# Gate and up weights of a fused S5 scan and gated MLP, loaded slot by slot over 128 partitions

## Chip, cores and metric

One core of one Trainium2 chip. The metric is the device time of one execution in microseconds; lower is better. Engines: PE is TensorE, DVE VectorE, ACT ScalarE, POOL GpSimd, SP SyncE, which computes nothing and issues most DMAs.

## What is computed

2048 tokens of 448 features are normalised; one branch is a diagonal complex recurrence (S5), the other a gated MLP, and both are multiplied and added to the input.

```python
xn = _layernorm(x)                                   # 2048 x 448
# S5: B_bar = ((Lam_bar - 1) / Lam) * (B_re + 1j B_im), 448 x 448
Bu = einsum("bld,pd->blp", xn, B_bar)
h[t] = Lam_bar * h[t-1] + Bu[t]
s = 2 * einsum("blp,dp->bld", h, Cmat).real + xn * Dskip
# MLP: w_gate, w_up 448 x 1792, w_down 1792 x 448
hid = sigmoid(xn @ w_gate) * (xn @ w_up)
g = silu(hid @ w_down)
out = x + s * g
```

All inputs and the output are bfloat16.

## The kernel before

**Tiling.** The tokens are 16 tiles of 128 (x tiles 0 to 15), worked in four chunks of 512. For a chunk the normalised x is transposed, features on partitions: chunk 0 on TensorE, chunks 1 to 3 by DMA transposes issued from SyncE. 448 features are seven slots of 64 rows. `wgt["g"]` and `wgt["u"]` (wG and wU in the profile) hold w_gate and w_up as [128 partitions, 7 slots, 896 columns]: partitions 0 to 63 hold the left 896 of the 1792 columns, partitions 64 to 127 the right 896, and slot s the feature rows 64 s to 64 s + 63. The 896 columns are seven column groups m of 128.

**The MLP's first products.** `gu_mm(c, k, m, ...)` (line 797) makes one column group of one chunk: for each of seven steps a pair of matmuls with 64 rows each, one on the lower partitions with slot s, one on the upper with slot s + 1 (modulo 7). `gu_evac` takes gate groups through a tanh on ACT, and up groups through a product on DVE (line 844) into hF. For chunk 0 the gate groups 0 and 1 are made tile by tile (`last_tile`, lines 825 and 826), then gate groups 2 to 6, then up groups 0 to 6, then the B products of the recurrence.

**Loads.** They stand in SyncE's queue in the order of the code: the x tiles 0 to 3 (two of them on ACT's queue), four loads of gate groups 0 and 1 (`load_w0`), then `load_w` for the rest. One `load_w` covers 64 partitions, seven slots and two or three column groups; groups 2 to 6 of the gate are four such loads (lines 418 to 421), the up weights are six (lines 432 to 438), with x tiles 4, 5 and 6, 7 between them. Then come four DMA transposes of B (`b_load`, line 742: for the real and the imaginary part one of 384 rows into bT 0 to 2, key bT, and one of 128 rows into bT 3, key bT3), dbc (the skip vector), the four transposes of chunk 1, w_down, the transposes of C, x tiles 8 to 15. GpSimd copies parts of bT into bT6 and bT's slot 3 (lines 746 to 754).

**B products.** `b_phase(c)` (line 870) makes four column groups. `pairs` are matmuls on slot 3 alone (bT3), `fulls` on slots 0 to 2; the group pt = 3 reads bT6 in place of bT.

**Order.** The program records every operation with its engine, an estimated cost and the keys it reads and writes; `Plan.solve` simulates backward and forward and emits the operations in order of planned start. TensorE's and the loads' order is as written (`chain`); DVE, ACT and POOL are ordered by the plan. `land` is the landing time that the plan assumes for a load, `HEAD_DMA` the number of DMAs at the head for which a fixed place among eight semaphores is assumed: DMA n waits for the landing of DMA n - 8. None of this sets a time on the chip; it sets the order. The waits between instructions follow from what each reads and writes: a matmul waits for the loads of the bytes that it reads.

**The end.** `yout` makes an output tile of a chunk in acc, DVE finishes it, `store` sends it from SyncE; `last_yout` is the last tile.

The new weight keys of the change are ("w", k, "s", s), one for a slot; `wkeys` (line 381) names what a column group reads for the plan.

Of the kernel before, what the change touches and what calls it, by code (L numbers as in the profile page):

```python
# [18 lines left out]
D = 448  # L19
F = 1792  # L20
P = 128
H = 64
# [4 lines left out]
TPC = L // P  # L27
NTAB = L + 1
EPS = 1e-5
HEAD_DMA = 19  # L30
TWO_PI = 2.0 * math.pi
PI = math.pi
MAGIC = 12582912.0
# [213 lines left out]
def kernel(  # L247
# [18 lines left out]
    V, A, G, T, Q = nc.vector, nc.scalar, nc.gpsimd, nc.tensor, nc.sync  # L266
# [99 lines left out]
    def load_w(eng, k, half, b, r=(), rate=105e3, land=0.0):  # L366
        m0, m1 = BLK[k][b]
        ps = slice(half * H, half * H + H)
        c0 = half * 896
        load(eng, [("w", k, half, m) for m in range(m0, m1)], H * 7 * (m1 - m0) * P * 2,  # L370
             wgt[k][ps, :, m0 * P:m1 * P],
             wsrc[k][:, c0 + m0 * P:c0 + m1 * P].rearrange("(s p) f -> p s f", p=H), cost=0.65, r=r, rate=rate, land=land)

    def load_w0(eng, half, part, r=(), land=0.0):
        ps = slice(half * H, half * H + H)
        s0, c0 = (1 - half if part == "A" else half), half * 896
        n = 4 - s0
        load(eng, [("w", "g", half, m, part) for m in range(2)], H * n * 2 * P * 2, wgt["g"][ps, s0:7:2, 0:2 * P],
             wsrc["g"][:, c0:c0 + 2 * P].rearrange("(s p) f -> p s f", p=H)[:, s0:7:2, :], cost=0.5, r=r, rate=400e3, land=land)

    def wkeys(k, m, part=None):
        if k == "u" or m > 1:
            return [("w", k, 0, m), ("w", k, 1, m)]
        if part == "b":
            return [("w", k, 0, m, "A"), ("w", k, 1, m, "A")]
        return [("w", k, h, m, q) for h in range(2) for q in "AB"]
# [14 lines left out]
    def load_p(eng, k, r=()):  # L401
# [13 lines left out]
    add("POOL", 0.15, lambda: G.memset(ident[:], 0.0), w=["ident"], chain=True)  # L415
    add("POOL", 0.4, lambda: G.affine_select(out=ident[:], in_=ident[:], compare_op=ALU.not_equal, fill=1.0, base=0,
                                             pattern=[[-1, P]], channel_multiplier=1), r=["ident"], w=["ident"], chain=True)
    load_w("SP", "g", 0, 1, rate=400e3, land=8.5)
    load_w("SP", "g", 1, 1, rate=400e3, land=9.5)
    load_w("SP", "g", 0, 2, rate=400e3, land=11.0)  # L420
    load_w("SP", "g", 1, 2, rate=400e3, land=12.4)
    load_x(4, 2, land=13.8)
    add("POOL", 0.1, lambda: G.memset(halfc[:], 0.5), w=["consts"])
    add("POOL", 0.1, lambda: G.memset(negc[:], -1.0), r=["consts"], w=["consts"])
    add("POOL", 0.1, lambda: G.memset(expc[:], math.e), w=["expc"])
# [3 lines left out]
                                    allow_small_or_imprecise_dtypes=True), w=[("wv", 0)])  # L429
    add("POOL", 0.15, lambda: G.memset(flat(g_raw[:, 512:2048], 3, 512)[:, :, D:512], 0.0),  # L430
        w=[("xnw", t) for t in (1, 2, 3)])
    load_w("SP", "u", 0, 0, rate=400e3, land=15.6)
    load_w("SP", "u", 1, 0, rate=400e3, land=16.8)
    load_x(6, 2, land=17.9)
    load_w("SP", "u", 0, 1, rate=400e3, land=19.0)
    load_w("SP", "u", 1, 1, rate=400e3, land=20.1)
    load_w("SP", "u", 0, 2, rate=400e3, land=21.6)
    load_w("SP", "u", 1, 2, rate=400e3, land=23.1)


    def warm_mm(n, w=512):
        def f():
            for _ in range(n):
# [167 lines left out]
    def xr(c, lo=0, hi=TPC):  # L611
        return [("xnT", c % 3, j, h) for j in range(lo, hi) for h in "ab"]
# [127 lines left out]
        add("POOL", 0.2, lambda: G.tensor_copy(out=sa7[H:P, :], in_=C("n2r")[H:P, 3:4]), r=["n2r"], w=["sa7b"])  # L740

    def b_load():
        for i, m in enumerate((A_B_re, A_B_im)):
            tload([("bT", i)], bT[:, 0:3, i, :], m[:, 0:384], D * 768, land=25.0 + 1.7 * i)
            tload([("bT3", i)], bT[:, 3:4, i, :], m[:, 320:448], D * 256, land=25.7 + 2.0 * i)
            add("POOL", 0.7, lambda i=i: G.tensor_copy(out=bT6[:, 0:3, i * H:i * H + H], in_=bT[:, 0:3, i, 384:448]),
                r=[("bT", i)], w=[("bT6", i)])
            if i == 0:
                add("POOL", 0.45, lambda: G.tensor_copy(out=bT[0:H, 3, 0, :], in_=bT[H:P, 3, 0, :]),
                    r=[("bT3", 0)], w=["bT3l"])  # L750
            for h in range(2):
                add("POOL", 0.25, lambda i=i, h=h: G.tensor_copy(out=bT6[h * H:h * H + H, 3, i * H:i * H + H],
                                                                        in_=bT[H:P, 3, i, 384:448]),
                    r=[("bT3", i)], w=[("bT6", i, h)])

    def c_load():
        for i, m in enumerate((A_C_re, A_C_im)):
# [112 lines left out]
    def b_phase(c, mid=None):  # L870
        x = xnT[c % 3]
        slots = [next_gu() for _ in range(3)]
        a3 = (next_acc(), next_acc())
        bk = [("bT", 0), ("bT", 1), ("bT3", 0), ("bT3", 1), "bT3l"]
        bk6 = [("bT6", 0), ("bT6", 1)] + [("bT6", i, h) for i in range(2) for h in range(2)]
        rs = [(slice(0, H), SL[6]), (slice(H, P), SL[5])]

        def halfrows(pt, start):
            for i, (hs, s_) in enumerate(rs):
                if pt < 3:  # L880
                    T.matmul(gu[slots[pt]][:, i, :], lhsT=bT[hs, 3, i, pt * P:pt * P + P], rhs=x[hs, s_, :],  # L881
                             start=start, stop=not start)
                else:
                    T.matmul(acc[a3[i]][:, 0:256], lhsT=bT6[hs, 3, :], rhs=x[hs, s_, i * 256:i * 256 + 256],
                             start=start, stop=not start)

        def pairs():
            for pt in (3, 0, 1) if c else (0, 1, 3):
                halfrows(pt, True)

        def fulls(pt, first):
            for i in range(2):
                for kt in range(3):
                    if pt < 3:
                        T.matmul(gu[slots[pt]][:, i, :], lhsT=bT[:, kt, i, pt * P:pt * P + P], rhs=x[:, kt, :],  # L895
                                 start=(first and kt == 0), stop=(not first and kt == 2))
                    else:
                        T.matmul(acc[a3[i]][:, 0:256], lhsT=bT6[:, kt, :],  # L898
                                 rhs=x[:, kt, i * 256:i * 256 + 256], start=False, stop=(kt == 2))

        def key(pt):
            return [("gu", slots[pt])] if pt < 3 else [("acc", a) for a in a3]

        def evac(pt):
            u = bus_n[0] % NBUS
            bus_n[0] += 1
            bus_of[c, pt] = u
            if pt < 3:
                add("ACT", act(1024), lambda: A.copy(out=bus[u][:], in_=gu[slots[pt]][:]), r=key(pt), w=[("bus", u)])  # L909
                return  # L910
            for i in range(2):
                ns = slice(i * 256, i * 256 + 256)
                for h, (d, q, l) in enumerate(((slice(0, P), slice(0, P), 0), (slice(0, H), slice(H, P), 1),
                                               (slice(H, P), slice(0, H), 1))):
                    add("ACT", 0.36, lambda ns=ns, d=d, q=q, l=l, i=i: A.copy(out=bus[u][d, l, ns], in_=acc[a3[i]][q, 0:256]),  # L915
                        r=[("acc", a3[i])] + ([("bus", u, i, 0)] if h else []),
                        w=[("bus", u) if h == i == 0 else ("bus", u, i, h)])

        add("PE", 0.54, pairs, r=xr(c) + bk + bk6, w=key(3) + key(0) + key(1), name=f"bp{c}")
        for pt in (3, 0, 1):  # L920
            add("PE", (1.29 if pt < 3 else 0.66) + (SW if pt == 3 else 0), lambda pt=pt: fulls(pt, False),
                r=xr(c) + bk + bk6 + key(pt), w=key(pt), name=f"b{c}.{pt}")
            evac(pt)
        if mid:
            mid([None, *((("gu", a), gu[a][:, 0, 0:D]) for a in slots[:2]), None])
        add("PE", 1.29, lambda: fulls(2, True), r=xr(c) + bk, w=key(2), name=f"b{c}.2")
        add("PE", 0.22 + SW, lambda: halfrows(2, False), r=xr(c) + bk + key(2), w=key(2), name=f"bp{c}.2")
        evac(2)

    bus_of = {}  # L930
# [127 lines left out]
    def yout(c, j, first=False):  # L1058
        t = c * TPC + j
        g, o, q = gt_of[c, j], next_o(), t % NXD  # L1060
        a = next_acc()
        key, ok, od = ("acc", a), ("o", o, 0), o_t[o][:]
        y = y_mm(c, j, acc[a], key, 0, D, False, first)
        add("DVE", dve1(D), lambda: V.tensor_tensor(out=od, in0=y, in1=xd[q][:], op=ALU.add), r=[key, ("xd", q)], w=[ok])
        add("DVE", dve2(D), lambda: V.tensor_tensor(out=od, in0=od, in1=g_t[g][:], op=ALU.mult), r=[ok, ("gt", g)], w=[ok])
        add("DVE", dve2(D), lambda: V.tensor_tensor(out=od, in0=od, in1=x_all[:, t, :], op=ALU.add), r=[ok, ("x", t)], w=[ok])
        rows = (0, H, P) if c == 2 and j == 3 else (0, P)
        for r0, r1 in zip(rows, rows[1:]):
            store(t, od, 0, D, r0, r1, [ok])

# [84 lines left out]
    gu_mm(0, "g", 3, None, 0, TPC, False)  # L1155
    gu_evac(0, "g", 3, None)
    b_load()
    load("SP", "dbc", P * D * 2, dbc[:], A_Dskip.unsqueeze(0).to_broadcast((P, D)), rate=400e3, land=29.0)

    def stats_for(c):  # L1160
        for t in range(4 * c, 4 * c + 4):
# [103 lines left out]
```

## Time and profile before

| what | us |
|---|---|
| median of 3 runs | 182.97 (182.96 to 183.09) |
| the profiled execution | 183.62 |
| its span, first to last instruction | 181.8 |
| TensorE busy | 176.3 |
| VectorE busy | 166.4 |
| ScalarE busy | 98.1 |
| GpSimd busy | 37.2 |
| DMA bytes | 13.43 MB in 30852 packets |

The profile page gives busy time by engine, the span in 40 slices of 4.5 us (each digit is a tenth; DMA is the mean share of the core's 16 DMA engines), the packets by queue, the chain of work that ended last, the costliest groups of instructions and the DMA issues with the time to landing. In a row such as `L807 PE MATMUL gu<-xnT,wU 64*128 64x512 bf16 x196` stand the line, the engine, what is written and read, and shapes. PEld is the weight load of TensorE, "SPq" an instruction of SyncE's queue. A share of DMA engines over 1 means that packets overlap on an engine.

The weight loads in today's page, with KB of one and the median time from issue to landing:

| loads | KB | us to landing |
|---|---|---|
| wG, two on SyncE | 224 | 4.8 |
| wG, two on SyncE | 336 | 6.4 |
| wU, four on SyncE | 224 | 9.6 |
| wU, two on SyncE | 336 | 9.2 |
| x tiles 4, 5 and 6, 7 | 224 | 7.2 |

### The profile page before, as it was taken

What the parts mean: (1) busy time and instruction counts of PE and PEld (TensorE: products, weight loads), DVE (VectorE), ACT (ScalarE), POOL (GpSimd) and SP (SyncE); (2) the same over time, 40 slices, a digit from 0 to 9 for tenths busy, and PEclk for the clock granted to TensorE, in tenths of its full rate; (3) what the DMA queues carried; (4) which work ended last, traced back from release to release, by engine and by line L of the source; (5) the groups of instructions that cost most, each with busy time, mean ns of one, the idle gap of its engine ahead of it and who ended that gap; (6) DMA issues with size and microseconds to landing.
All of it is one profiled execution on the core that took longest, in us unless ns stands there. A gap on an engine that the chain in (4) does not pass through costs nothing.

```text
span 181.8 us, 3610 instructions
## 1 busy us (share of the span) xinstructions
PE 176.3 (97%) x1404; PEld 88.0 (48%) x1411; DVE 166.4 (92%) x294; ACT 98.1 (54%) x162; POOL 37.2 (20%) x93
## 2 busy tenths in 40 slices
PE   8899998999999999999999999999999999999993
PEld 2764444564544444445554444444555444455552
DVE  3866889999989999999999999999999999999772
ACT  4999899958699985364145543348210533411101
POOL 6463556200008797000004100000000000000000
PEclk9999999999999999999999999999999999999999
DMA  5899989999200290000004900001000000002111
GB/s 129 234 216 217 171 159 183 258 251 226 72 0 0 50 140 15 0 4 0 0 2 82 134 14 0 4 0 62 14 4 0 25 27 26 3 0 76 58 54 48
DMA packets 30852, 13.43 MB, mean 74 GB/s; under 512 B 19441, under 2 KB 30834, under 8 KB 30834
## 3 DMA queue, kind: packets, MB, share of 16 engines
q1 hardware_dynamic: 30208, 12.83, 35.0%
q10 hardware_dynamic: 562, 0.36, 0.7%
q8 instruction: 11, 0.18, 0.4%
q14 instruction: 7, 0.06, 0.1%
q0 software_dynamic: 64, 0.00, 0.0%
HBM read 6.77 MB, written 1.84 MB: 47 GB/s over the span
## 4 chain that ended last, share of the span: by engine, by line
PE 81%; DMA 6%; DVE 4%; SPq 4%; ACT 2%; issue 1%; DVEq 0%
PE gu L807 34%; PE gu L1023 15%; PE acc L1042 11%; PE acc L1023 9%; PE gu L895 8%; DMA x_all<-in_A_x_dram 6%; SPq L357 4%; DVE hF L844 2%; PE acc L898 2%; PE gu L881 2%; ACT hT L680 1%; ACT xn L534 1%; DVE bst L450 1%; PE gu L808 1%; DVE spm L687 0%
## 5 line engine op out<-in xcount | busy, mean ns | idle before, releaser
L807 PE MATMUL gu<-xnT,wU 64*128 64x512 bf16 x196 | 45.8, 376 | 0.0
L808 PE MATMUL gu<-xnT,wU 64*128 64x512 bf16 x196 | 45.8, 376 | 0.0
L807 PE MATMUL gu<-xnT,wG 64*128 64x512 bf16 (+1 forms) x189 | 41.3, 360 | 0.0
L808 PE MATMUL gu<-xnT,wG 64*128 64x512 bf16 (+1 forms) x189 | 41.3, 360 | 0.0
L841 ACT ACTIVATE sig<-gu 128x1024 f32<-128x1024 f32 x21 | 21.3, 1019 | 24.7 <-PE gu L808 20.1
L1023 PEld LDWEIGHTS <-hF 128*128 128x128 bf16 x224 | 21.9, 98 | 20.6
L807 PEld LDWEIGHTS <-wU 64*128 64x128 bf16 x196 | 18.4, 94 | 22.9
L807 PEld LDWEIGHTS <-wG 64*128 64x128 bf16 x196 | 18.4, 94 | 19.9
L1023 PE MATMUL gu<-wd,hF 128*128 128x448 bf16 x140 | 28.0, 352 | 0.0
L844 DVE SCALAR_TENSOR_TENSOR hF<-sig,gu 128x1024 bf16<-128x1024 f32 x21 | 25.4, 1210 | 0.7 <-ACT sig L841 0.4
L1042 PE MATMUL acc<-cT,hT 128*128 128x448 bf16 (+2 forms) x119 | 22.9, 337 | 0.0
L962 DVE TENSOR_TENSOR_SCAN wv<-c_r,st,z 128x512 bf16<-128x512 f32 x18 | 22.8, 1273 | 0.0
L1029 ACT ACTIVATE g_t<-gu 128x448 bf16<-128x448 f32 x10 | 5.4, 540 | 27.7 <-PE gu L1023 16.8
L808 PEld LDWEIGHTS <-wU 64*128 64x128 bf16 x196 | 18.4, 94 | 0.0
L808 PEld LDWEIGHTS <-wG 64*128 64x128 bf16 x196 | 18.4, 94 | 0.0
L1023 PE MATMUL acc<-wd,hF 128*128 128x448 bf16 x84 | 16.9, 352 | 0.0
L1042 PEld LDWEIGHTS <-hT 128*128 128x128 bf16 x126 | 11.6, 98 | 9.9 <-issue 0.4
L895 PE MATMUL gu<-xnT,bT 128*128 128x512 bf16 x65 | 15.3, 379 | 0.4
L909 ACT CAST bus<-gu 128x1024 bf16<-128x1024 f32 x12 | 12.0, 1011 | 5.9 <-PE gu L881 5.3
L540 POOL COPY xn<-xn 128x448 bf16<-128x448 bf16 x12 | 7.5, 627 | 28.8 <-ACT xn L534 28.6
L450 DVE BATCH_NORM_STATS2 bst<-x_all 128x6 f32<-128x448 bf16 x11 | 6.4, 616 | 5.8 <-DMA x_all<-in_A_x_dram 5.8
L915 ACT CAST bus<-acc 64x256 bf16<-64x256 f32 (+1 forms) x24 | 8.7, 368 | 4.8 <-PE acc L898 4.4
(161 smaller groups left out, 264.1 us busy)
## 6 DMA issues: line engine op xcount, KB each, us to landing
wd<-in_B_w_down_dram SPq DMA_DIRECT2D x2, 784.0 KB, 6.4
out_dram<-o_t SPq DMA_DIRECT2D x14, 112.0 KB, 1.7
wU<-in_B_w_up_dram SPq DMA_DIRECT2D x4, 224.0 KB, 9.6
x_all<-in_A_x_dram SPq DMA_DIRECT2D x2, 448.0 KB, 5.0
wG<-in_B_w_gate_dram SPq DMA_DIRECT2D x2, 336.0 KB, 6.4
wU<-in_B_w_up_dram SPq DMA_DIRECT2D x2, 336.0 KB, 9.2
wG<-in_B_w_gate_dram SPq DMA_DIRECT2D x2, 224.0 KB, 4.8
x_all<-in_A_x_dram SPq DMA_DIRECT2D x2, 224.0 KB, 7.2
```

The costliest lines, as they stand in the source:

```text
L450: add("DVE", 0.56 if t < TPC else 0.6, lambda: V.bn_stats(out=bst[b][:], in_=x_all[:, t, :]), r=[("x", t)] + ([("xnT", 0, 3, "a")] if 3 < ...
L540: add("POOL", 0.25 if n == H else 0.6, lambda: G.tensor_copy(out=o[:, D:D + n], in_=o[:, 0:n]), r=[("xn", b)], w=[("xnw", b)])
L807: T.matmul(bank[0][:, ts], lhsT=w_[0:H, s, ms], rhs=x[0:H, SL[s], ts], start=(s == 0), stop=(s == 6))
L808: T.matmul(bank[1][:, ts], lhsT=w_[H:P, (s + 1) % 7, ms], rhs=x[H:P, SL[s], ts], start=(s == 0), stop=(s == 6))
L841: add("ACT", act(1024), lambda: A.activation(th, gu[a][:], ACT.Tanh, scale=0.5), r=[("gu", a)], w=[tk])
L844: add("DVE", dve1(1024), lambda: V.scalar_tensor_tensor(out=ho, in0=th, scalar=1.0, in1=gu[a][:], op0=ALU.add, op1=ALU.mult), r=[("gu", a) ...
L895: T.matmul(gu[slots[pt]][:, i, :], lhsT=bT[:, kt, i, pt * P:pt * P + P], rhs=x[:, kt, :], start=(first and kt == 0), stop=(not first and k ...
L909: add("ACT", act(1024), lambda: A.copy(out=bus[u][:], in_=gu[slots[pt]][:]), r=key(pt), w=[("bus", u)])
L915: add("ACT", 0.36, lambda ns=ns, d=d, q=q, l=l, i=i: A.copy(out=bus[u][d, l, ns], in_=acc[a3[i]][q, 0:256]), r=[("acc", a3[i])] + ([("bus" ...
L962: dve(1.194, lambda k=k: V.tensor_tensor_scan(out=wv[:, k, :], data0=rb, data1=z[:, k, :], initial=(st[pt][:, k, :] if c else 0.0), op0=AL ...
L1023: T.matmul(d, lhsT=hF[c % 2][:, m, h, js], rhs=wd[:, ft, :], start=(ft == 0), stop=(ft == FT - 1))
L1042: T.matmul(y, lhsT=hT[c % 2][:, hm, js], rhs=cT[:, cm, c0:c1], start=(i == 0 and not skip_on_pe), stop=(i == 6))
```

## The change

The four later gate loads become seven, one for a slot: `load_rows` writes columns 256 to 895 of slot s on all 128 partitions in one DMA. The source is the 64 feature rows of the slot, with the two column halves as the leading dimension. The six up loads become seven in the same way, all 896 columns each. x tiles 4 to 7 stand between the gate and the up loads. In `b_load` the two transposes of 128 rows go ahead of those of 384, and the GpSimd copies follow them; `b_phase` names for each column group only the parts of B that it reads. Every tile of chunk 2 and the last of chunk 1 is stored in two halves of 64 rows. Assumed landings and `HEAD_DMA` are set anew.

```diff
-HEAD_DMA = 19
+HEAD_DMA = 25
...
+    def load_rows(eng, k, s, m0, m1, land=0.0):
+        src = wsrc[k][s * H:s * H + H, :].rearrange("p (h f) -> h p f", h=2)[:, :, m0 * P:m1 * P]
+        load(eng, ("w", k, "s", s), P * (m1 - m0) * P * 2, wgt[k][:, s, m0 * P:m1 * P], src, cost=0.45, rate=400e3, land=land)
...
     def wkeys(k, m, part=None):
         if k == "u" or m > 1:
-            return [("w", k, 0, m), ("w", k, 1, m)]
+            return [("w", k, "s", s) for s in range(7)]
...
-    load_w("SP", "g", 0, 1, rate=400e3, land=8.5)
-    load_w("SP", "g", 1, 1, rate=400e3, land=9.5)
-    load_w("SP", "g", 0, 2, rate=400e3, land=11.0)
-    load_w("SP", "g", 1, 2, rate=400e3, land=12.4)
-    load_x(4, 2, land=13.8)
+    for s in range(7):
+        load_rows("SP", "g", s, 2, 7, land=7.7 + 0.5 * s)
+    load_x(4, 2, land=11.6)
+    load_x(6, 2, land=12.4)
+    for s in range(7):
+        load_rows("SP", "u", s, 0, 7, land=13.2 + 0.7 * s)
...
-    load_w("SP", "u", 0, 0, rate=400e3, land=15.6)
-    load_w("SP", "u", 1, 0, rate=400e3, land=16.8)
-    load_x(6, 2, land=17.9)
-    load_w("SP", "u", 0, 1, rate=400e3, land=19.0)
-    load_w("SP", "u", 1, 1, rate=400e3, land=20.1)
-    load_w("SP", "u", 0, 2, rate=400e3, land=21.6)
-    load_w("SP", "u", 1, 2, rate=400e3, land=23.1)
...
     def b_load():
-        for i, m in enumerate((A_B_re, A_B_im)):
-            tload([("bT", i)], bT[:, 0:3, i, :], m[:, 0:384], D * 768, land=25.0 + 1.7 * i)
-            tload([("bT3", i)], bT[:, 3:4, i, :], m[:, 320:448], D * 256, land=25.7 + 2.0 * i)
-            add("POOL", 0.7, lambda i=i: G.tensor_copy(out=bT6[:, 0:3, i * H:i * H + H], in_=bT[:, 0:3, i, 384:448]),
-                r=[("bT", i)], w=[("bT6", i)])
+        src = (A_B_re, A_B_im)
+        for i in range(2):
+            tload([("bT3", i)], bT[:, 3:4, i, :], src[i][:, 320:448], D * 256, land=19.8 + 1.3 * i)
...
+        for i in range(2):
+            tload([("bT", i)], bT[:, 0:3, i, :], src[i][:, 0:384], D * 768, land=22.6 + 1.7 * i)
+            add("POOL", 0.7, lambda i=i: G.tensor_copy(out=bT6[:, 0:3, i * H:i * H + H], in_=bT[:, 0:3, i, 384:448]),
+                r=[("bT", i)], w=[("bT6", i)])
...
-        bk = [("bT", 0), ("bT", 1), ("bT3", 0), ("bT3", 1), "bT3l"]
-        bk6 = [("bT6", 0), ("bT6", 1)] + [("bT6", i, h) for i in range(2) for h in range(2)]
+        bh = [("bT3", 0), ("bT3", 1), "bT3l"]
+        bh6 = [("bT6", i, h) for i in range(2) for h in range(2)]
+        bk = {pt: [("bT", 0), ("bT", 1)] if pt < 3 else [("bT6", 0), ("bT6", 1)] for pt in range(4)}
...
-        rows = (0, H, P) if c == 2 and j == 3 else (0, P)
+        rows = (0, H, P) if c == 2 or (c == 1 and j == 3) else (0, P)
...
-    load("SP", "dbc", P * D * 2, dbc[:], A_Dskip.unsqueeze(0).to_broadcast((P, D)), rate=400e3, land=29.0)
+    load("SP", "dbc", P * D * 2, dbc[:], A_Dskip.unsqueeze(0).to_broadcast((P, D)), rate=400e3, land=26.5)
```

More of the change, by code (lines that the diff above doesn't have):

```diff
@@ L917, in evac @@
                         w=[("bus", u) if h == i == 0 else ("bus", u, i, h)])
-        add("PE", 0.54, pairs, r=xr(c) + bk + bk6, w=key(3) + key(0) + key(1), name=f"bp{c}")
+        add("PE", 0.54, pairs, r=xr(c) + bh + bh6, w=key(3) + key(0) + key(1), name=f"bp{c}")
         for pt in (3, 0, 1):
             add("PE", (1.29 if pt < 3 else 0.66) + (SW if pt == 3 else 0), lambda pt=pt: fulls(pt, False),
-                r=xr(c) + bk + bk6 + key(pt), w=key(pt), name=f"b{c}.{pt}")
+                r=xr(c) + bk[pt] + key(pt), w=key(pt), name=f"b{c}.{pt}")
             evac(pt)
@@ L925, in b_phase @@
             mid([None, *((("gu", a), gu[a][:, 0, 0:D]) for a in slots[:2]), None])
-        add("PE", 1.29, lambda: fulls(2, True), r=xr(c) + bk, w=key(2), name=f"b{c}.2")
-        add("PE", 0.22 + SW, lambda: halfrows(2, False), r=xr(c) + bk + key(2), w=key(2), name=f"bp{c}.2")
+        add("PE", 1.29, lambda: fulls(2, True), r=xr(c) + bk[2], w=key(2), name=f"b{c}.2")
+        add("PE", 0.22 + SW, lambda: halfrows(2, False), r=xr(c) + bh + key(2), w=key(2), name=f"bp{c}.2")
         evac(2)
```

## Prediction

> **What bounds the kernel now.** I read the page first (busy shares and slices), then busy time by stretch, the chain of waits, and the DMA queues by stretch.
>
> ```profile
> PE 176.3 (97%) x1404; PEld 88.0 (48%) x1411; DVE 166.4 (92%) x294; ACT 98.1 (54%) x162; POOL 37.2 (20%) x93
> ...
> PE   8899998999999999999999999999999999999993
> ...
> DMA  5899989999200290000004900001000000002111
> ```
>
> TensorE is busy in every slice; the DMA engines are full only in the first ten slices (45 us). So a faster load can win only where TensorE stands idle, and a slower one costs in full once TensorE runs out of weights.
>
> ```profile
> 10.30:17.70 7.40, 7.40 (x78) 3.41 (x74) 5.03 (x13) 7.32 (x9) 3.51 (x6) 1.00 1.18 217
> 17.70:28.30 10.60, 10.60 (x100) 4.77 (x98) 8.90 (x15) 9.77 (x19) 5.34 (x12) 1.00 1.02 158
> 28.30:29.30 1.00, 0.61 (x6) 0.26 (x3) 0.98 (x2) 1.00 (x4) 0.62 (x3) 1.00 1.23 180
> ```
>
> In each row: stretch, length, PE, PEld, DVE, ACT, POOL busy, clock, DMA share, GB/s. The gate columns 2 to 6 of chunk 0 fill 10.3 to 17.7, the up columns 17.7 to 28.3, both without a gap: no load is late today. The one hole is 0.39 us after 28.3, before the B matmuls. The chain of waits (start, length) tells where it comes from:
>
> ```profile
> 8.53 10.21 DMA x_all<-in_A_x_dram
> 18.74 0.02 issue
> 18.76 1.15 DVE bst L450 x2
> ...
> 28.13 1.14 DVE hF L844
> 29.27 0.04 issue
> 29.32 0.39 PE gu L881 x2
> ```
>
> Tiles 6 and 7 of x land at 18.74, their statistics start late on VectorE, and its hF products run until B's banks come free. That hole is all that earlier loads could earn.
>
> **The change, part by part.** *What is removed:* ten weight loads onto 64 partitions (four gate, six up), 512 or 768 bytes a packet. *What comes:* seven gate loads of 128 rows of 1280 bytes and seven up loads of 128 rows of 1792 bytes. Bytes are the same. SyncE issues them at 0.62 us each, four more than before (2.5 us, beside TensorE's work).
>
> What each costs hangs on how many DMA engines share it. The destination leads with 128 partitions, the source with a dimension of 2 (the column halves, 64 rows in each). In every load of today's trace both sides lead with the same count, so no row tells which decides. What the trace does show is ACT's queue in the first 6 us (packets, MB, share; then its issues):
>
> ```profile
> q10 hardware_dynamic: 562, 0.36, 20.6%
> ...
> x_all<-in_A_x_dram ACTq DMA_DIRECT2D x2, 112.0 KB, 2.5
> wG<-in_B_w_gate_dram ACTq DMA_DIRECT2D x1, 128.0 KB
> hF<-in_A_Lambda_re_dram ACTq DMA_DIRECT2D x1, 0.9 KB
> ```
>
> Data packets: 128 + 128 rows of x, 256 gate rows of 512 bytes, one row of 896 bytes, 513 in all. The other 49 are completions: 16 + 16 + 16 + 1. A load that leads with 64 or 128 is finished by 16 engines; the one that leads with 1 by one engine, in one packet, though its 896 bytes could have been cut. So a load is cut along its leading dimension alone. To give each engine a slice of both sides, a source that leads with 2 can be cut in two. I take **two engines**; the other end, sixteen, is a rival below.
>
> The Trainium skill, "DMA: Bandwidth & Descriptors", section "Why a DMA increments its semaphore by 16 and not by 1", states this as a rule: the largest number up to 16 that divides the slowest dimension of both sides. By that rule it is two engines here, and the 16 + 16 + 16 + 1 above agrees; no load in this trace has unequal sides.
>
> Price of a packet, from two stretches with one packet size (22.6 to 23.2, the transposes' 256 bytes; 35 to 37, w_down's 896 bytes):
>
> ```profile
> q1 hardware_dynamic: 694, 0.17, 128.5%
> ```
>
> ```profile
> q1 hardware_dynamic: 845, 0.74, 107.8%
> ```
>
> Share x 16 engines x length / packets: 1.285 x 16 x 600 / 694 = 17.8 ns, and 1.078 x 16 x 2000 / 845 = 40.8 ns. The line through both is 0.0359 ns per byte: 54.6 ns for 1280 bytes, 73.0 for 1792. An engine moves 64 packets of each load: 3.49 us per gate load, 4.67 per up load. Seven of each, plus the 2 x 16 packets of the x loads between them (1.3): 24.4 + 32.7 + 1.3 = 58.4 us on the two engines, one load behind the other.
>
> Start: the last gate load of columns 0 and 1 is issued at 3.07 and the fastest gate load lands 3.7 later, 6.8. The last gate load then lands at about 31.2, x tiles 4 to 7 at 32.5, the last up load at **65.2**. SyncE issues load n when load n-8 has landed, which keeps the two engines fed: up load 6 needs x tile 4 (31.9), long before its turn at 60.5.
>
> What waits: each matmul pair waits for its own slot, so gate column 2 can't end before 31.2, and up column 0 not before 65.2. The five gate columns, hidden today, lie in the wait for the up loads. After 65.2 TensorE has 0.3 us left of column 0 and six columns: 10.6 / 7 = 1.51 each, 9.1. The up columns end at 74.6 against 28.3: **+46.3**. All that follows is TensorE-bound and moves with it.
>
> *The clock.* TensorE would come out of 25 us with a pair of matmuls every 4.7 us. The nearest row is its cold start:
>
> ```profile
> 2.42 0.15 PEld L444 LDWEIGHTS <-const-bfloat16-1.0 128*128 128x128 bf16 x1 [0.27 <-issue]
> 2.85 0.15 PEld L444 LDWEIGHTS <-const-bfloat16-1.0 128*128 128x128 bf16 x1 [0.28 <-issue]
> 3.28 0.15 PEld L444 LDWEIGHTS <-const-bfloat16-1.0 128*128 128x128 bf16 x1 [0.28 <-issue]
> ```
>
> Warm-up matmuls of 512 columns start 0.43 apart until 3.7; in the steady stages they start 0.21 apart. Eight spacings of 0.21 lost are **+1.7** (bounds 0 and 2.1, ten matmuls).
>
> *What VectorE gains:* tables and statistics are done during the wait, so the hole at 28.3 goes: **-0.4**.
>
> *B's transposes and bT6 copies.* Order small, small, big, big, and the pair matmuls wait for the small ones alone. All four stand behind the up loads in the queue. Today B's four land within 6 us of the last up load (22.6; POOL's wait for the last ends at 28.5); after, by 71.2, and POOL's bT6 copies (0.35 each) end by 72. TensorE gets to B at 74.6 + 1.7 = 76.3. Priced at nothing, with 4 us to spare; if the cover goes, what B is late. Behind them, dbc (VectorE queues the skip products, and behind these the last hF, on it) lands 6.6 after the last up load today, so 71.8, before hF column 5 is done at 76. The transposes of chunk 1 land 11.5 after it today, 76.7, against a need at 83. GpSimd's copies of xn stand behind the small transposes' copies, ready at 69.
>
> *Stores.* Five more, each half of a tile. SyncE waits 62 us in all for VectorE before stores, and the last tile's stores are unchanged: nothing (at worst two store issues, 0.7).
>
> *Sum:* 46.3 + 1.7 - 0.4 = +47.6. The profiled run took 183.62, 181.8 in the span and 1.8 around it; the median of the runs is 182.97. On the median: **230.6**.
>
> Its bounds. Below: if only bytes count (0.0359 ns each, nothing per packet), 14 loads take 49.4 instead of 57.1, and the clock stays up: 230.6 - 7.7 - 1.7 = 221. Above: 896-byte price per byte (0.0455 ns), 62.6, +5.5, and each load leaving its engine idle for one issue, 14 x 0.62 = 8.7: 245. The contended price (64-partition loads, 222 GB/s from 10 to 16) doesn't apply: fourteen engines are idle.
>
> **The rivals.**
>
> *Sixteen engines, not slower.* If the destination's 128 partitions decide, a gate load is 8 packets of 54.6 ns an engine, 0.44 us, less than its issue. For it speaks that today's loads onto 64 partitions run at 222 GB/s and w_down onto 128 at 370.
>
> ```profile
> 34.60:36.60 2.00, 2.00 (x40) 1.76 (x38) 1.90 (x4) 1.51 (x3) 0.00 (x0) 1.00 1.08 370
> 10.00:16.00 6.00, 6.00 (x73) 2.93 (x68) 4.38 (x11) 5.97 (x8) 2.96 (x6) 1.00 1.16 222
> ```
>
> Issue then sets the pace: from 3.86, where the first removed gate load is issued, at 0.62 + 0.04 each, gate load 6 lands at about 10.7 (needed five sevenths into column 2, 11.4), the last up load is issued at 14.0 and lands before 17.7. x tiles 6 and 7 land some 7 us earlier, the 0.39 hole closes, nothing else can: 182.6, between 182.0 (the 0.07 idle in B too, and a little from the tail) and 183.4 (a late gate load). Against it: the single-row load. It decides from the point where a row load posts 16 completions instead of 2.
>
> The Trainium skill's "Rules for kernel authors" on the same page also speaks for one 128-partition transfer over two halves; the 222 and 370 GB/s agree with it.
>
> *Two engines with gaps.* If on an engine a load starts only when the one before has landed, each adds about 2.0 us (an x tile lands 2.3 after issue, 0.3 of it transfer): 14 x 2.0 = +28, 259. Against it: today's queue shows no such gaps, 1.16 busy from 10 to 16.
>
> *One engine.* If the leading 2 isn't cut: 57.1 more, 288.
>
> **How the numbers follow.** Two engines 0.79, gaps 0.03, one engine 0.02, sixteen 0.16. Predicted is the likeliest, 230.6; its own range is 221 to 245. To hold 8 in 10 the range goes to 219 and to 260, which takes in the gaps. No change is within 0.2% of 182.97 (0.37 us), about what a measurement can tell. Sixteen engines at 182.6 sits on that edge: 0.09 faster, 0.05 same, 0.02 slower; all else is slower: 0.86.
>
> **What would show it.** Right: the slices show DMA at one tenth from 7 to 65 us, near 50 GB/s; SyncE's queue has 14 x (128 + 2) packets for the weights; TensorE idles from 10 to 31 and from about 40 to 65; x tile 4 lands at 32, the up columns end near 76. Wrong: 370 GB/s before 15 us and no hole in TensorE (sixteen engines); an up load every 6.7 us (gaps) or 9.3 us (one engine). If DMA is as said and the end is not, the covers behind 65 us failed: then B's matmuls or the skip products wait.

## The result and the profile after

The changed kernel takes **229.81 us** (median of 6 runs, 228.63 to 230.85) where the kernel before took 183.05 on the same chip (6 runs, 182.96 to 183.35): a ratio of **1.254 [1.250, 1.259]**, 46.8 us more. The forecast was 230.6. The profiled execution took 229.93 us, 228.2 of it in the span, against 183.62 and 181.8 before.

From the page of the changed kernel, TensorE's busy share first, then the slices of 5.7 us each and all packets:

```profile
PE 185.4 (81%) x1404; PEld 89.6 (39%) x1411; DVE 165.7 (73%) x294; ACT 98.3 (43%) x162; POOL 34.5 (15%) x93
...
PE   8912258021189999999999999999999999999994
...
PEclk9965559855559999999999999999999999999999
DMA  5111311111999991000900000830001000000221
...
DMA packets 28096, 13.43 MB, mean 59 GB/s; under 512 B 19373, under 2 KB 28078, under 8 KB 28078
```

The DMA row, full in the first ten slices before, stands at one tenth in most slices from 6 to 57 us. TensorE's row has two holes, and its clock row falls to five tenths in and behind both. From slice 14 on TensorE is busy throughout, as before.

Busy time by stretch of the changed kernel (stretch, length, PE, PEld, DVE, ACT, POOL, clock, DMA share, GB/s):

```profile
10.30:32.00 21.70, 5.08 (x37) 1.41 (x33) 1.86 (x5) 3.47 (x5) 1.56 (x3) 0.58 0.20 68
32.00:40.00 8.00, 7.09 (x56) 2.81 (x52) 4.96 (x18) 5.61 (x7) 3.12 (x6) 0.87 0.14 53
40.00:64.00 24.00, 3.02 (x12) 0.65 (x14) 0.00 (x0) 10.39 (x22) 0.00 (x0) 0.59 0.46 58
```

The first hole is the wait for the gate slots (5.08 us busy out of 21.70), then the gate columns run, then the second hole is the wait for the up slots (3.02 out of 24.00). The table of waits names them (waiter, what for, us in all, times, the longest):

```profile
PEld L806 <- DMA wU<-in_B_w_up_dram: 24.7, 6, 4.4
PE gu L806 <- DMA wU<-in_B_w_up_dram: 21.9, 6, 4.1
...
PE gu L806 <- DMA wG<-in_B_w_gate_dram: 16.6, 6, 2.9
```

Six waits each, one for each slot but the first, the longest about as long as a load less a pair of matmuls. The chain of waits (start, length, what) shows that these loads set the end:

```profile
42.44 4.41 SPq L357
46.89 16.87 DMA wU<-in_B_w_up_dram
63.81 0.61 PE gu L806
64.42 0.42 PE gu L806
...
68.26 0.25 PE gu L806
68.51 0.21 PE gu L806
...
75.63 0.33 PE gu L880 x4
```

The last up load was issued at 46.89 and landed 16.87 us later. Its matmuls start 0.42 us apart until 68.26 and 0.21 after that: half clock first. Busy time by stretch shows it in the clock (the number after POOL's):

```profile
63.80:68.30 4.50, 4.49 (x22) 1.67 (x24) 1.59 (x2) 0.00 (x0) 3.51 (x10) 0.51 1.27 201
68.30:75.30 7.00, 7.00 (x68) 3.11 (x66) 6.07 (x8) 0.00 (x0) 3.08 (x17) 1.00 0.98 208
```

B comes at 75.63 in the chain; before, its matmuls behind the hole came at 29.32. From there to the end of the span it is 152.57 us, and it was 152.48 before: **all but 0.1 of the 46.4 us of span stand ahead of B.**

In the stretch from 54.9 to 56.4, where a single up load is moving, the DMA queues read:

```profile
q1 hardware_dynamic: 42, 0.08, 12.9%
```

42 packets of 1792 bytes in 1.5 us at 50 GB/s. A packet took 74 ns by the trace's records, so 42 x 74 / 1500 is 2.07 engines at work, of 16.

### The profile page after: what moved, and what is told of

Same layout as the page of the kernel before. It is cut to its first block, busy times and chain, and to the rows that moved or that the text cites. A ratio compares the mean times of both kernels' runs of the same rounds, so it can differ in the third digit from the quotient of the medians.

```text
span 228.2 us, 3621 instructions
## 1 busy us (share of the span) xinstructions
PE 185.4 (81%) x1404; PEld 89.6 (39%) x1411; DVE 165.7 (73%) x294; ACT 98.3 (43%) x162; POOL 34.5 (15%) x93
## 2 busy tenths in 40 slices
DMA packets 28096, 13.43 MB, mean 59 GB/s; under 512 B 19373, under 2 KB 28078, under 8 KB 28078
## 4 chain that ended last, share of the span: by engine, by line
PE 70%; SPq 20%; DMA 7%; issue 1%; DVE 1%; DVEq 0%
PE gu L805 27%; SPq L357 20%; PE gu L1022 12%; PE acc L1041 9%; DMA wU<-in_B_w_up_dram 7%; PE acc L1022 7%; PE gu L894 7%; PE gu L806 6%; PE acc L897 1%; PE gu L880 1%; DVE o_t L1083 0%; DVE o_t L1077 0%; PE acc L883 0%; PE acc L1039 0%; DVEq L1083 0%
## 5 line engine op out<-in xcount | busy, mean ns | idle before, releaser
L806 PE MATMUL gu<-xnT,wU 64*128 64x512 bf16 x196 | 49.7, 394 | 21.9 <-DMA wU<-in_B_w_up_dram 21.9
L806 PE MATMUL gu<-xnT,wG 64*128 64x512 bf16 (+1 forms) x189 | 43.7, 369 | 16.6 <-DMA wG<-in_B_w_gate_dram 16.6
L805 PE MATMUL gu<-xnT,wU 64*128 64x512 bf16 x196 | 49.9, 394 | 0.0
L805 PE MATMUL gu<-xnT,wG 64*128 64x512 bf16 (+1 forms) x189 | 43.7, 367 | 0.1
L806 PEld LDWEIGHTS <-wU 64*128 64x128 bf16 x196 | 18.9, 97 | 31.3 <-DMA wU<-in_B_w_up_dram 24.7
L842 DVE SCALAR_TENSOR_TENSOR hF<-hF,gu 128x1024 bf16<-128x1024 bf16 x7 | 8.5, 1221 | 30.6 <-issue 27.9
L806 PEld LDWEIGHTS <-wG 64*128 64x128 bf16 x196 | 18.8, 96 | 23.8 <-DMA wG<-in_B_w_gate_dram 19.4
L805 PEld LDWEIGHTS <-wU 64*128 64x128 bf16 x196 | 18.9, 97 | 17.1
L805 PEld LDWEIGHTS <-wG 64*128 64x128 bf16 x196 | 18.8, 96 | 16.2 <-DMA wG<-in_B_w_gate_dram 0.2
L1041 PE MATMUL acc<-cT,hT 128*128 128x448 bf16 (+2 forms) x119 | 22.9, 337 | 0.0
L839 ACT ACTIVATE hF<-gu 128x1024 bf16<-128x1024 f32 x6 | 6.0, 1021 | 20.6 <-PE gu L806 20.6
```

Source lines behind the costliest of these rows:

```text
L805: T.matmul(bank[0][:, ts], lhsT=w_[0:H, s, ms], rhs=x[0:H, SL[s], ts], start=(s == 0), stop=(s == 6))
L806: T.matmul(bank[1][:, ts], lhsT=w_[H:P, (s + 1) % 7, ms], rhs=x[H:P, SL[s], ts], start=(s == 0), stop=(s == 6))
L839: add("ACT", act(1024), lambda: A.activation(th, gu[a][:], ACT.Tanh, scale=0.5), r=[("gu", a)], w=[tk])
L842: add("DVE", dve1(1024), lambda: V.scalar_tensor_tensor(out=ho, in0=th, scalar=1.0, in1=gu[a][:], op0=ALU.add, op1=ALU.mult), r=[("gu", a) ...
L1041: T.matmul(y, lhsT=hT[c % 2][:, hm, js], rhs=cT[:, cm, c0:c1], start=(i == 0 and not skip_on_pe), stop=(i == 6))
```

## The experiments

**How many engines: 4, 8 or 128 ahead in the source.** The three kernels change one line of the changed kernel, the pattern by which a slot load reads (other rows, so other values are multiplied; same packets, same bytes):

```
-src = wsrc[k][s * H:s * H + H, :].rearrange("p (h f) -> h p f", h=2)[:, :, m0 * P:m1 * P]
+src = wsrc[k].rearrange("(a q) f -> a q f", a=4)[:, s * 11:s * 11 + 32, m0 * P:m1 * P]     # lead4
+src = wsrc[k].rearrange("(a q) f -> a q f", a=8)[:, s * 6:s * 6 + 16, m0 * P:m1 * P]       # lead8
+src = wsrc[k][s * H:s * H + H, :].rearrange("p (h f) -> (p h) f", h=2)[:, m0 * P:m1 * P]   # lead128
```

> The changed kernel with one edit: the source of a slot load leads with 128 (row and column half merged) in place of 2; same destination, same bytes, same row lengths. The weights stand interleaved on the partitions, so the products are of other values. Theory (the smaller leading count sets the number of DMA engines): sixteen engines, up loads landed before 18 us, no wait on TensorE, 182.6 us. Rival (the 1280 and 1792 byte rows or one slot per load are slow by themselves, whatever the source): about 230 as the changed kernel.

> As the changed kernel, but a slot load's source leads with 4 (four groups of 32 other weight rows, same row lengths and counts, so other values are multiplied). Theory: four engines, each load takes half as long (1.66 and 2.26 us), last up load lands near 36, up columns end 46 to 48, time 200 to 203. Rival (only 1, 2 or 16 engines are possible, or the destination decides): 230 or 183.

> As the changed kernel, but a slot load's source leads with 8 (eight groups of 16 other weight rows, so other values are multiplied). Theory: eight engines, 0.83 and 1.13 us a load, last up load lands near 22.5, up column 0 ends 3.6 us late, time 186. Rival (the destination decides or the form of three dimensions is slow): 230 or 183.

Measured: 183.16 us with 128 ahead (ratio 1.0004 [0.9994, 1.0013]), 202.86 with 4 (1.108 [1.105, 1.110], two runs), 187.52 with 8 (1.023 [1.021, 1.025]). Expected were 182.6, 200 to 203 and 186; why the last missed by 1.5 us stays open. The last up packet starts at 17.6, 36.5 and 22.9 us, with 2 ahead at 63.2. TensorE's and the DMA engines' slices and the packets, from the page with 4 ahead:

```profile
PE   8943972699999999999999999999999999999993
...
DMA  5243239899970000930000058000010000001221
...
DMA packets 28124, 13.43 MB, mean 67 GB/s; under 512 B 19401, under 2 KB 28106, under 8 KB 28106
```

with 8 ahead:

```profile
PE   8969799999999999999999999999999999999993
...
DMA packets 28180, 13.43 MB, mean 72 GB/s; under 512 B 19457, under 2 KB 28162, under 8 KB 28162
```

and with 128 ahead:

```profile
PE   8999999999999999999999999999999999999993
...
DMA  4999999993000390000004900002000000002221
...
DMA packets 28292, 13.44 MB, mean 74 GB/s; under 512 B 19569, under 2 KB 28274, under 8 KB 28274
```

The weights come in the same data packets in all four kernels, so what differs between the totals is completions. Against the 28096 of the changed kernel they are 28, 84 and 196 more: 14 x (4 - 2), 14 x (8 - 2) and 14 x (16 - 2). A slot load posts 2, 4, 8 or 16 completions, as many as engines share it, while its destination leads with 128 partitions every time. The smaller leading dimension decides here; a source that leads with more than its destination, or with a count that is no power of two, was not tried.

The Trainium skill, "DMA: Bandwidth & Descriptors", section "Why a DMA increments its semaphore by 16 and not by 1", says that the engines of a transfer are the largest number up to 16 that divides the slowest dimension of both sides. These four kernels agree, with unequal sides, which the trace before could not show.

**One kind of load alone.** The first kernel keeps the gate slots and puts the old up loads back, the second keeps the up slots and puts the old gate loads back:

```
+    load_w("SP", "u", 0, 0, rate=400e3, land=15.6)      # gate_slots: six of these for the seven
...
-        load_rows("SP", "u", s, 0, 7, land=13.2 + 0.7 * s)
+    load_w("SP", "g", 0, 1, rate=400e3, land=8.5)       # up_slots: four of these for the seven
...
-        load_rows("SP", "g", s, 2, 7, land=7.7 + 0.5 * s)
```

> The changed kernel with only the gate loads by slot, the up loads as before. Theory: gate slot 6 lands near 31, gates end near 39, up loads are there by then (their shares on the two engines wait behind the gate's), 204 us. Rival (the two waits add up to 47, so the gate's part is 20 by bytes): 203, not told apart by time, but then the two runs sum to 47, not to 51. Rival: gate loads are hidden, 183.

> The changed kernel with only the up loads by slot, the gate loads as before. Theory: seven loads of 4.52 from 14.5 on two engines, last lands near 46.7, up columns end near 58.5, 213 us. Rival (by bytes of the sum): 210. Rival: hidden, 183.

Measured: 206.12 and 211.82 us, one run each, with the kernel before at 183.18. The waits of the kernel with gate slots alone, and of the one with up slots alone:

```profile
PE gu L810 <- DMA wG<-in_B_w_gate_dram: 17.6, 6, 3.6
```

```profile
PE gu L808 <- DMA wU<-in_B_w_up_dram: 23.7, 6, 4.1
```

The two cost 22.9 and 28.6 us by themselves, 51.5 in all as the theory had it (51; the rival 47), and 46.8 together. That 4.7 are missing fits TensorE's work on the gate columns, which lies in the wait for the up loads when both are there. That it is all of the 4.7 is not shown: with gate slots alone the last gate slot's first matmul came at 32.57, 1.7 us later than in the changed kernel (30.88).

**The rest of the change alone.** Old weight loads, with the new order of B's transposes, its split waits, the half-tile stores, and planned landings set to the old loads:

```
-            tload([("bT", i)], bT[:, 0:3, i, :], m[:, 0:384], D * 768, land=25.0 + 1.7 * i)
+            tload([("bT3", i)], bT[:, 3:4, i, :], src[i][:, 320:448], D * 256, land=24.0 + 1.3 * i)
...
-        rows = (0, H, P) if c == 2 and j == 3 else (0, P)
+        rows = (0, H, P) if c == 2 or (c == 1 and j == 3) else (0, P)
```

> The change without the slot loads: gate and up weights loaded as before; B's two small transposes first, keys of B by part, split stores; planned landings set to the old loads. Theory (these parts lie under other work): 183.0, within 0.4 of before. Rivals: the earlier small transposes shorten the hole before B, 182.6; the split stores lie on the end, 183.7.

Measured: 183.31 against 183.18 us, ratio 1.0012 [1.0000, 1.0025]. These parts cost at most 0.25%. Busy time by stretch of this kernel, at the place of the hole:

```profile
28.30:29.30 1.00, 1.00 (x12) 0.48 (x9) 0.81 (x2) 1.00 (x4) 0.92 (x7) 1.00 1.45 190
```

TensorE is busy all through it (0.61 us before), yet the time did not fall. The kernel with 128 ahead closed the hole as well (1.00 of 1.00) and did not get faster either.

**The clock.** The changed kernel with matmuls of constants added in the wait of up column 0. First 18 of them after pairs 2, 3 and 4, into a bank of acc:

```
+                if c == 0 and k == "u" and m == 0 and s in (2, 3, 4):
+                    for _ in range(18):
+                        T.matmul(acc[0][:], lhsT=ones[:, 0:P], rhs=ones[:, 0:512], start=True, stop=True)
```

> The changed kernel with 18 idle matmuls on constants after each of the pairs 2, 3 and 4 of up column 0, where TensorE waits for the next slot; acc 0 is overwritten where it is free. Theory (half clock after the wait costs eleven spacings of 0.21): TensorE at full clock when the last slot lands, 227.5 us. Rival (the slow matmuls after the wait have another cause): 229.8 or more.

Measured: 228.54 us (4 runs, 227.86 to 230.23), 1.3 less than the changed kernel. The added matmuls wrote over a bank that gate column 3 of chunk 0 still held, so that column has other values and ScalarE's work on it came late; the size of the gain couldn't be read from it. The next kernel wrote into a bank of gu that the pair after next overwrites, after pairs 1 to 4, beside the changed kernel once more:

```
+                if (c, k, m) == (0, "u", 0) and s in (1, 2, 3, 4):
+                    for _ in range(18):
+                        T.matmul(gu[(a + 1) % 3][:, 0, :], lhsT=ones[:, 0:P], rhs=ones[:, 0:512], start=True, stop=True)
```

> The changed kernel with 18 matmuls of constants more after each of pairs 1, 2, 3 and 4 of up column 0, into the bank of gu that the pair after next will overwrite; no value of the output changes. Theory (TensorE's matmuls run at half clock from 63.8 to 68.3 us of the changed kernel because it was nearly idle before, and that stands on the path): matmuls 0.21 us apart from the last up load on, up columns end some 1.9 us earlier, 2.2 us less than the changed kernel on the same chip, about 227.6. Rival (the clock's loss is hidden behind B's transposes or given back later): up columns end earlier but the time stays within 0.5 of the changed kernel's, 229.3 to 230.3.

> The changed kernel again, unaltered, as the measure for the run with the added matmuls on this chip: 229.8, as before.

Measured: 229.41 us (6 runs) and 229.97 (6 runs). The gain missed what was expected: 0.6, not 2.2. The trace shows why: 18 matmuls a pair are more than fit between two loads, and the last slot's first matmul started at 65.69 instead of 63.82, 1.87 us late, which gave the gain back. So 14 in their place (`range(14)`):

> The run with added matmuls again, 14 instead of 18 after each of pairs 1 to 4, since 18 of them ran on past the last up load (the last slot's first matmul came at 65.7 instead of 63.8); the values stay the reference's. Theory (the half clock after the loads stands on the path): 14 take some 5 us at half clock after pair 1 and 3.0 at full clock after the others, so TensorE is free by about 63 when the last up load lands near 63.8, matmuls are 0.21 apart from there, the up columns end 1.9 to 2.2 earlier than in the changed kernel and the time is 227.5 to 228.0 (against 229.8 and 230.0 of the changed kernel). Rival (given back later): 229.3 to 230.3.

Measured: 227.77 us (6 runs, 227.07 to 228.62), **2.0 and 2.2 less** than the changed kernel's two medians. It ran on another chip than the second of them; the kernel before took 183.20 beside it, and 183.05 and 183.18 beside the two. TensorE's timeline of this kernel (start, length, line, operation, count, idle time before it):

```profile
59.63 3.23 PE L810 MATMUL gu<-const-bfloat16-1.0 128*128 128x512 bf16 x13
62.80 0.39 PE L805 MATMUL gu<-xnT,wU 64*128 64x512 bf16 x1
63.85 0.39 PE L806 MATMUL gu<-xnT,wU 64*128 64x512 bf16 x1 [0.67 <-DMA wU<-in_B_w_up_dram]
63.85 0.39 PE L805 MATMUL gu<-xnT,wU 64*128 64x512 bf16 x1
64.08 0.38 PE L806 MATMUL gu<-xnT,wU 64*128 64x512 bf16 x1
```

and its chain of waits at B:

```profile
73.31 0.21 PE gu L806
73.52 0.33 PE gu L885 x4
```

The last load lands when it did (63.85 against 63.81), the matmuls behind it come 0.21 us apart at once, and B starts at 73.52 instead of 75.63: 2.11 earlier for more work on TensorE. The half clock behind the wait stood on the path.

The Trainium skill, "TensorE: Matmul & The Clock Gate", section "Part 1: The HAM clock gate", says that the array goes to half rate after an idle window of some 3.4 us and back after a busy one, and that the windows run freely. By that rule the half-rate time after a wait would vary with where the window lies; here it lasted 4.45 us in the changed kernel's profile (63.81 to 68.26) and about 3.1 in its second one (63.82 to 66.9). That agrees; the windows themselves are in no trace here.

**Can the loads be saved?** Two other ways to issue them. In the kernel before, the halves of the up weights that go to partitions 64 to 127 were issued from GpSimd's queue, the others from SyncE's:

```
-    load_w("SP", "u", 1, 0, rate=400e3, land=16.8)
...
+    for b in range(3):
+        load_w("POOL", "u", 1, b, r=["turn"])
```

> The kernel before, with the three up loads of partitions 64 to 127 issued from GpSimd's queue in place of SyncE's, so that packets to the two halves of the partitions can interleave on each engine. Theory (what can be won is the hole of 0.39 us before B): up loads faster than 222 GB/s and x tiles 6 and 7 earlier, 182.6. Rivals: the halves share the same engines and nothing moves, 183.0; GpSimd's issue delays its small operations, above 183.4.

Measured: 183.87 against 183.18 us, ratio 1.0033 [1.0015, 1.0050]: 0.3% longer, and not the 182.6 expected. Its busy time by stretch, and one of its waits:

```profile
10.30:17.70 7.40, 7.40 (x82) 3.49 (x78) 4.67 (x13) 7.32 (x9) 5.39 (x12) 1.00 1.16 205
17.70:28.30 10.60, 10.39 (x97) 4.51 (x95) 9.52 (x17) 10.21 (x20) 6.30 (x16) 1.00 1.12 170
```

```profile
PEld L805 <- DMA wU<-in_B_w_up_dram: 0.7, 1, 0.7
```

Two queues moved 205 GB/s where one moved 217 before, and 170 where it moved 158 in the next stretch; over both (10.3 to 28.3) it is 184 against 183. TensorE's weight loads now waited 0.7 us for an up load, its matmuls 0.21. GpSimd issued that load at 9.39, where SyncE had issued it at 7.86, so the later issue alone could be the cause; that this wait makes the whole 0.7 of the time was not tried.

In the changed kernel, each slot load was cut into two loads of 64 partitions, whose sources lead with 64:

```
-        load(eng, ("w", k, "s", s), P * (m1 - m0) * P * 2, wgt[k][:, s, m0 * P:m1 * P], src, cost=0.45, rate=400e3, land=land)
+        for h in range(2):
+            load(eng, ("w", k, "s", s, h), H * (m1 - m0) * P * 2, wgt[k][h * H:h * H + H, s, m0 * P:m1 * P], src[h], cost=0.65, rate=400e3, land=land + 0.6 * s)
```

> The changed kernel with each of its 14 slot loads issued as two loads of 64 partitions each, whose source leads with 64 instead of 2. Theory (engines go by the leading dimension of the source, 64 gives sixteen): every engine takes part, and the price left is that of 14 issues more on SyncE's queue, some 0.65 us each, so the last up load lands near 25 instead of 63, and up column 0 ends some 5 to 6 us later than before the change: 188 to 189. Rival 1 (the number of slots sets two engines, however it is cut): 230. Rival 2 (the issues are hidden): 183.

Measured: 191.91 us (4 runs, 190.99 to 192.93), ratio 1.049 [1.046, 1.053]. Of the 46.8 us, 38 are gone. The packets are 420 more than the changed kernel's 28096, which is 28 x 16 - 14 x 2 completions, so every engine takes part; the price left is 8.7 and not the 5 to 6 expected. Here are the packets from its page, and SyncE's issues and TensorE's last wait for an up load from its timelines:

```profile
DMA packets 28516, 13.44 MB, mean 71 GB/s; under 512 B 19793, under 2 KB 28498, under 8 KB 28498
```

```profile
1.64 11.58 SPq L357 DMA_DIRECT2D wG<-in_B_w_gate_dram  x17
13.27 1.10 SPq L357 DMA_DIRECT2D x_all<-in_A_x_dram  x2
14.41 9.02 SPq L357 DMA_DIRECT2D wU<-in_B_w_up_dram  x14
```

```profile
26.45 0.39 PE L807 MATMUL gu<-xnT,wU 64*128 64x512 bf16 x1 [1.36 <-DMA wU<-in_B_w_up_dram]
```

Issue sets the pace: 28 slot loads at about 0.60 us each, the last one at 22.61. Its data came by 24.9 as expected, but its matmul started at 26.45, and B at 35.7 (28.5 before). That is 7.2 of the 7.4 us that the span grew. Of the load's sixteen completions fifteen came by 25.39 and the last at 26.41, so one engine's was a microsecond late. Why it was, and why two of the other three runs are 1.7 and 1.9 above the profiled one, stays open.

None of these kernels beats the kernel before.

## Why the prediction was right, point by point

**Two engines** was the step on which all hung, argued from one load of a single row that posts one completion. It held: 2.07 engines busy in the trace, and 2, 4, 8 and 16 completions in the experiments. The sixteen-engine rival fell with its condition. Its price was off by little: with sixteen engines the time is 183.16, not 182.6.

**The price of a packet** was 54.6 and 73.0 ns and measured 55 and 74. What the step missed is that an engine overlaps its packets a little: they start 51.9 and 70.6 ns apart, so a gate load took 3.32 us (3.49 said) and an up load 4.52 (4.67), 2.2 us less for the fourteen. The first gate packet also starts at 5.77, where 6.8 was taken as the start. Against these stand the packets of the first gate load and of the last up load, spread over 4.32 and 4.84 us, and half a microsecond from the last up packet (63.2) to the last slot's first matmul (63.8). The forecast was 65.2: **the loads were 1.4 us too dear in the sum**, by errors of both signs.

**The covers.** Statistics of x tiles 4 and 5 start at 31.43, said for 31.9 to 32.5. The two costs overlap as said: the gate columns run while the up loads are under way (51.5 against 46.8). The up columns end at 75.5, said for 76.3.

**The clock** was sized at 1.7 with a bound of 2.1 and measured 2.1 (B 2.11 earlier without it, the time 2.0 to 2.2 less). The mechanism was right. The row of the cold start gave eight spacings; in this execution it was ten, and in the second profile of the same kernel seven (some 1.5 us), so the size of the term varies from one execution to the next.

**The hole of 0.4** closes in the trace as said, but two kernels that close it alone gain nothing in their medians (1.0004 and 1.0012). The profiled execution before was itself 0.6 us above its median, so whether its other executions had that hole is open. That term of the sum is not borne out.

**SyncE's queue** was told wrongly in part. The prediction said that it issues load n when load n-8 has landed. The trace shows another thing, below: the issue itself lasts, and it runs two to three loads ahead (the last up load's issue starts at 46.89, when the fourth of the seven is moving). B's four transposes do stand behind the up loads, as said, and were through sooner: GpSimd's last bT6 copy ended at 68.5 (72 said), and TensorE, which got to B at 75.6, did not wait for them. The price of nothing was right, with more to spare.

**The rest at nothing** (order of the transposes, split waits, stores): 1.0012 [1.0000, 1.0025] alone.

The errors: -1.4 for the loads, +0.4 for the clock, and some -0.2 in where the columns begin and end. That is -1.2 in the span, 229.4 said and 228.2 measured. On the medians it is -0.8 (230.6 against 229.81); the 0.4 taken off for the hole, which is not borne out, brings the forecast nearer by luck.

## What to carry to other kernels

Before merging loads into one wide transfer, read the leading dimension of both sides: in these kernels the smaller one set the number of engines (2, 4 or 8, and 16 for 64 and 128), and 128 partitions at the destination do not help a source rearranged to lead with 2. Count completions in the trace: they tell how many engines the loads use. And when TensorE must wait long for data, add the half clock that follows the wait to the price (1.5 to 2.1 us here), or give it idle work that fits into the gaps.

## What the runs showed that was not expected

**Once the engines are behind, most issues last about as long as a load.** From the chain of waits of the changed kernel, SyncE's own queue:

```profile
6.91 3.86 SPq L357
10.82 3.73 SPq L357
14.60 3.22 SPq L357
...
37.98 4.41 SPq L357
42.44 4.41 SPq L357
```

Each issue took 0.4 to 0.8 us until 5 us. From 6.91 on most took about as long as a load takes on its two engines (3.32 and 4.52), though the second x load and the first up load took 0.8 again. SyncE issued nothing else in that time, and x tiles 4 and 5 came to be issued only at 21.13.

**A transpose's packets start before the loads ahead of it are done, but it lands behind them.** SyncE's timeline of the changed kernel:

```profile
51.34 6.58 SPq L398 DMA_TRANSPOSE bT<-in_A_B_re_dram  x1
57.97 1.65 SPq L398 DMA_TRANSPOSE bT<-in_A_B_im_dram  x1
59.66 4.10 SPq L398 DMA_TRANSPOSE bT<-in_A_B_re_dram  x1
63.81 1.43 SPq L398 DMA_TRANSPOSE bT<-in_A_B_im_dram  x1
```

Packets of 256 bytes, the transposes' size, moved from 56.5 us on, seven microseconds before the last up load was done, some 470 of them by 60. But the first of GpSimd's copies that waits for a transpose starts at 64.37, behind the last up load (63.8). That the early packets ran on engines that the up loads left idle is likely, but not shown: the trace names no engine for a packet. The issues of the four took 1.43 to 6.58 us; what held the long ones was not tried.

**Halves from two queues are not faster than from one**: 184 GB/s against 183 over 10.3 to 28.3 us of the same kernel. The Trainium skill, "DMA: Bandwidth & Descriptors", section "Rules for kernel authors", says of two transfers to disjoint partition halves that they share the same engines and aren't worth it; this run agrees.
